# A two-layer decode kernel: three transposing K transfers put ahead of the K loads

## The chip, the cores and the metric

The kernel runs on one core of a Trainium2 chip. The metric is the device time of one execution in microseconds (us). The profile's span runs from the first to the last instruction of a profiled execution and is a little shorter than that execution's device time.

The engines are named as in the profile: PE (TensorE matmul), PEld (its weight load), DVE (VectorE), ACT (ScalarE), POOL (GpSimd), SP (SyncE). SP computes nothing here; it issues every DMA of the kernel, and "SPq" in the profile is its queue. The transfers themselves run on the core's 16 DMA engines.

## The reference

Four sequences (B = 4) of one token each go through two layers, and both layers use the same weights and the same caches. A layer is grouped-query attention over a cache of 4096 positions, and then a gated unit:

```
x = x + A(layernorm(x))      # q = x wq ; softmax(q K^T / sqrt(128)) V ; o wo
x = x + B(layernorm(x))      # (sigmoid(x w_gate) * (x w_up)) w_down
x = x + A(layernorm(x))
x = x + B(layernorm(x))
```

There are 32 query heads and 8 K/V heads of 128 elements, D = 512, F = 1792, all in bf16. One K/V head of one sequence is 4096 x 128 bf16, which is 1 MB for K and 1 MB for V. The caches hold 32 such pairs, 64 MB in all, and layer two needs every one of them again.

## The kernel before

A **unit** is one (layer, sequence, K/V head). Units are worked in pairs: `seq` holds 64 units and the main loop at the end of the kernel runs over `plan`, one pair at a time. SBUF has `NSLOT = 12` **slots** of 1 MB (128 partitions x 4096 bf16). Each slot holds the K or the V of one unit. A K unit is loaded with row p of the slot holding positions 32p to 32p+31; DVE then turns it in place, in blocks of 32x32 words of 32 bits (`k_turn`, L923); `scores` (L940) multiplies the turned slot with the spread queries. `smax`, `spread_max` and `softmax` (L956, L965, L975, L983) make the probabilities, `ptrans` (L1000 to L1032) turns them, `pv` (L1048) multiplies them with V, and `wo_pair` (L1098) with the output weights. Some units of layer one stay in their slots for layer two (`RET`); the others are loaded a second time, so 104 slot loads are made.

All DMAs go out from SP in the order of the list `loads`. `pump()` takes the first free slot (`free`, a list that starts as 0 to 11) for each K or V load, and returns when no slot is free; weights (`wo`, `wg`, `wu`, `wd`) are in the same list and need no slot. Ahead of `loads` stand the load of x and four loads of wq (L394), 1 MB each. A small recorder (`_Sched`) derives the waits: whoever writes a key such as `s9` (slot 9) waits for its last writer and all its readers. A wait of a DMA is a wait of SP, and whatever stands behind it in SP's order waits too. Every slot has its own semaphore (`d0` to `d11`).

The order on SP at the start is: x, wq0 to wq3, K into slots 0 to 4, V into slot 5, one block of wo (512 KB), K into slot 6, V into slot 7, wo, two blocks of wg, K into slot 8, V into slot 9, wo, two blocks of wg, K into slot 10, V into slot 11. Only then do slots come round again.

At the start the compute engines do what needs no K: layernorm, masks, the query matmuls (L621, which wait for wq). Then DVE turns the first two K units, and behind the second turn on DVE stands the scaling of the queries (L632), which the first scores need.

Of the kernel before, what the change touches and what calls it, by code (L numbers as in the profile page):

```python
# [185 lines left out]
def bass_interleave_layers__gqa_block_cached__glu_gated_glu__decode_kernel(  # L186
# [17 lines left out]
    P = 128  # L204
# [4 lines left out]
    NJ = SK // P  # L209
# [12 lines left out]
    S = _Sched()  # L222
# [4 lines left out]
    def sbt(shape, dtype, name):  # L227
        cnt[0] += 1
        return es.enter_context(nc.sbuf_tensor(f"{name}_{cnt[0]}", list(shape), dtype))
# [4 lines left out]
    slot = [sbt([P, NJ * DH], dt.bfloat16, f"slot{i}") for i in range(NSLOT)]  # L234
# [127 lines left out]
    def pump():  # L362
        while loads:
            kind, n = loads[-1]
            if kind in wparts:
                loads.pop()
                dst, src = wparts[kind](n)
                S.dma("sp", (lambda dst, src: lambda e: e.dma_start(dst, src))(dst, src), f"wo{n}" if kind == "wo" else kind, writes=[f"{kind}{n}"])  # L368
                continue
            if not free:  # L370
                return
            loads.pop()
            s = take()
            _, b, u = seq[n]
            if kind == "k":
                where["kn", n] = s
                src = A_k_cache[b, u].rearrange("(p j) d -> p (j d)", p=P)
            else:
                where["v", b, u] = s
                src = A_v_cache[b, u].rearrange("(p j) d -> p (j d)", p=P)  # L380
            dst = slot[s][:, :]
            S.dma("sp", (lambda dst, src: lambda e: e.dma_start(dst, src))(dst, src), f"d{s}", writes=[f"s{s}"])  # L382
# [8 lines left out]
    for k in range(KD):  # L391
        S.dma(
            "sp",
            (lambda k: lambda e: e.dma_start(wq_sb[:, k, :], A_wq[k * P:(k + 1) * P, :]))(k),  # L394
            f"wq{k}",
            writes=[f"wq{k}"],
        )
    pump()

# [4 lines left out]
        writes=["pe0"],  # L404
    )
    dve(lambda e: e.transpose(pidx[:, :], iota_f[:, 0:32]), writes=["pe0"])
    for a in range(4):
# [6 lines left out]
            writes=[f"ident{a}"],  # L414
# [5 lines left out]
    for k in range(KD):  # L420
# [13 lines left out]
        writes=[f"x{b}" for b in range(Bn)],  # L434
# [705 lines left out]
    for b in range(Bn):  # L1140
        n = vstep[last[0, b]] - 1
# [155 lines left out]
```

## Time and profile before

| What | Value |
|---|---|
| median of 2 runs | 324.73 us (323.7 to 325.76) |
| profiled execution, device time | 326.53 us |
| its span | 324.7 us |
| mean granted TensorE clock | 0.686 of full speed |
| PE / DVE / ACT busy | 70% / 58% / 45% of the span |
| bytes moved by DMA | 123.63 MB, mean 381 GB/s |
| DMA queue of SP (q1) | 94.1% of 16 engines' span |
| slot loads | 56 of V and 48 of K, 1 MB each |

The busy shares are averages over stages with different limits. The row of the DMA queue counts the time that the packets took on the 16 engines. In the profile's slices each digit is a tenth of busy time in one of 40 equal parts of the span, some 8.1 us each.

### The profile page before, as it was taken

To read this page: it belongs to the slowest core of one execution; us is meant where nothing else is said; L and a number is where in the kernel's file an instruction comes from. 1 tells how busy PE (TensorE), PEld (TensorE's weight loads), DVE (VectorE), ACT (ScalarE), POOL (GpSimd) and SP (SyncE) were. 2 spreads that over 40 slices of the span, in tenths; PEclk is the share of its full clock that TensorE was granted. 3 is DMA by queue.
4 is the path that set the end of the run, shared out by engine and by line. 5 is a ranking of instruction groups with operands and counts; after the bars stand their busy time and mean duration, and the time that the engine had idled before them with its cause. 6 is when DMAs were issued, how large, how long until landed. Compare 5 with 4: busy or idle time off the path is not lost.

```text
span 324.7 us, 10428 instructions
## 1 busy us (share of the span) xinstructions
PE 227.0 (70%) x4408; PEld 157.4 (48%) x4408; DVE 188.0 (58%) x441; ACT 145.4 (45%) x600; POOL 12.8 (4%) x36
## 2 busy tenths in 40 slices
PE   1345523008197998768798986799797869878975
PEld 1313312006156465546556564464565646455865
DVE  6387343304656458865647696674886467475243
ACT  1005421205045276655435765543676653377620
POOL 0000000000000010000001000000100000010000
PEclk9999999999996655555765555555655555675555
DMA  7999999999999999999999999999999999999800
GB/s 277 428 422 411 401 404 400 401 386 390 400 406 376 339 376 425 418 422 418 410 370 377 417 424 421 421 388 380 377 421 419 420 422 422 417 416 419 369 18 3
DMA packets 22814, 123.63 MB, mean 381 GB/s; under 512 B 2024, under 2 KB 7920, under 8 KB 8944
## 3 DMA queue, kind: packets, MB, share of 16 engines
q1 hardware_dynamic: 22768, 122.96, 94.1%
q8 instruction: 35, 0.57, 0.7%
q14 instruction: 11, 0.09, 0.1%
HBM read 122.95 MB, written 0.00 MB: 379 GB/s over the span
## 4 chain that ended last, share of the span: by engine, by line
DMA 29%; PE 24%; issue 22%; DVE 12%; SPq 11%; ACT 1%; POOL 0%; DVEq 0%; POOLq 0%
DMA slot<-in_A_v_cache_dram 19%; PE O_ps L1048 7%; DVE slot L923 7%; SPq L382 6%; DMA wo<-in_A_wo_dram 5%; DMA slot<-in_A_k_cache_dram 5%; SPq L368 4%; PE S_ps L940 4%; PE O_ps L1098 3%; PE MS L965 2%; PE MS L1007 2%; PE M_ps L858 1%; DVE small L956 1%; PE M_ps L809 1%; PE PT L1000 1%
## 5 line engine op out<-in xcount | busy, mean ns | idle before, releaser
L1032 ACT ACTIVATE pT<-PT 32x64 bf16<-32x64 f32 x504 | 108.1, 214 | 55.1 <-PE PT L1000 43.6
L923 DVE STREAM_TRANSPOSE slot<-slot 128x2048 f32<-128x2048 f32 (+1 forms) x61 | 112.3, 1840 | 32.4 <-DMA slot<-in_A_k_cache_dram 32.4
L1048 PE MATMUL O_ps<-pT,slot 128*128 128x4 bf16 x2048 | 62.0, 166 | 26.3 <-DMA slot<-in_A_v_cache_dram 26.3
L1048 PEld LDWEIGHTS O_ps<-pT,slot 128*128 128x128 bf16 x2048 | 63.5, 105 | 29.8 <-DMA slot<-in_A_v_cache_dram 27.2
L940 PE MATMUL S_ps<-slot,qz 128*16 128x512 bf16 x512 | 59.4, 612 | 3.4 <-POOL qz L675 2.3
L983 ACT ACTIVATE pe<-S_ps,small 128x512 bf16<-128x512 f32 x32 | 22.0, 686 | 59.0 <-issue 40.4
L965 PE MATMUL MS<-valid_f,small 128*128 128x64 f32 x64 | 20.6, 422 | 22.4 <-DVE small L956 22.4
L1098 PEld LDWEIGHTS O_ps<-oT,wo 128*128 128x128 bf16 x640 | 19.3, 105 | 28.8 <-issue 28.4
L965 PEld LDWEIGHTS MS<-valid_f,small 128*128 128x128 f32 x64 | 15.0, 291 | 37.6 <-DVE small L956 34.1
L1098 PE MATMUL O_ps<-oT,wo 128*128 128x2 bf16 (+1 forms) x640 | 20.3, 166 | 16.7 <-DMA wo<-in_A_wo_dram 15.6
L956 DVE TENSOR_REDUCE small<-S_ps 128x1 f32<-128x512 f32 x32 | 21.2, 662 | 6.5 <-PE S_ps L940 6.5
L675 POOL TENSOR_TENSOR qz<-qc,small 128x128 bf16<-128x128 bf16 x32 | 12.6, 399 | 280.9 <-ACT qc L661 143.5
L940 PEld LDWEIGHTS S_ps<-slot,qz 128*16 128x16 bf16 x512 | 12.4, 109 | 22.8 <-issue 17.7
L1007 PE MATMUL MS<-head_f,small 128*128 128x8 f32 x64 | 17.9, 353 | 0.0
L1080 DVE TENSOR_TENSOR oT<-O_ps,rden 128x8 bf16<-128x8 f32 x32 | 5.2, 164 | 19.7 <-PE O_ps L1048 17.9
L1007 PEld LDWEIGHTS MS<-head_f,small 128*128 128x128 f32 x64 | 16.4, 314 | 0.0
L1015 DVE RECIPROCAL rden<-MS 128x8 f32<-128x8 f32 x32 | 6.6, 206 | 14.8 <-PE MS L1007 14.8
L975 DVE CUSTOM_DVE_ANT_0 junk<-MS,mask_f,small 128x64 bf16<-128x64 f32 x32 | 8.5, 267 | 11.4 <-PE MS L965 11.4
L1000 PE MATMUL PT<-ident_bf,pe 128*128 128x64 bf16 x128 | 12.0, 231 | 1.9 <-ACT pe L983 1.5
L1112 DVE TENSOR_TENSOR xT<-xT,O_ps 128x4 f32<-128x4 f32 x32 | 3.9, 154 | 16.1 <-PE O_ps L1098 16.0
L809 PE MATMUL M_ps<-wq,xc_bf 128*1 128x512 bf16 x128 | 12.9, 574 | 0.0
L661 ACT ACTIVATE qc<-M_ps 128x128 bf16<-128x128 f32 x8 | 1.9, 280 | 19.5 <-PE M_ps L650 19.5
(79 smaller groups left out, 150.3 us busy)
## 6 DMA issues: line engine op xcount, KB each, us to landing
slot<-in_A_v_cache_dram SPq DMA_DIRECT2D x56, 1024.0 KB, 11.0
slot<-in_A_k_cache_dram SPq DMA_DIRECT2D x48, 1024.0 KB, 11.7
wq<-in_A_wq_dram SPq DMA_DIRECT2D x4, 1024.0 KB, 7.8
wo<-in_A_wo_dram SPq DMA_DIRECT2D x8, 512.0 KB, 15.9
wg<-in_B_w_gate_dram SPq DMA_DIRECT2D x4, 448.0 KB, 14.0
wu<-in_B_w_up_dram SPq DMA_DIRECT2D x4, 448.0 KB, 14.4
wd<-in_B_w_down_dram SPq DMA_DIRECT2D x2, 896.0 KB, 16.6
row<-in_A_x_dram SPq DMA_DIRECT2D x1, 4.0 KB
```

The costliest lines, as they stand in the source:

```text
L382: S.dma("sp", (lambda dst, src: lambda e: e.dma_start(dst, src))(dst, src), f"d{s}", writes=[f"s{s}"])
L809: (lambda k, st: lambda e: e.matmul(M_ps[h][32 * st:32 * st + 1, :], lhsT=xc_bf[:, k, 0:1], rhs=wv[:, k, h, :, st, :], start=(k == 0), sto ...
L923: dve(lambda e: e.transpose(kf, kf), writes=[f"s{st}"])
L940: (lambda t, b2, e_, c, r0, ul: lambda e: e.matmul(S_ps[p][r0:r0 + 4 * REP, :], lhsT=qz_sb[p][:, ul, t, :, :].rearrange("p a r -> p (a r)" ...
L956: lambda e: e.tensor_reduce(rm_sb[p], S_ps[p][:, :], AX.X, ALU.max),
L965: lambda e: e.matmul(MS[:, 0:16 * REP], lhsT=rm_sb[p].broadcast_to([P, P]), rhs=valid_f[:, :], start=True, stop=True),
L983: lambda e: e.activation(pe_sb[p].rearrange("p j m -> p (j m)"), S_ps[p][:, :], ACTF.Exp, bias=nm_sb[p], scale=exp_scale, accum_out=sm_sb[ ...
L1000: (lambda j: lambda e: e.matmul(PT[:, j * 64:(j + 1) * 64], lhsT=pe_sb[p][:, j, :], rhs=valid_bf, start=True, stop=True))(j)
L1007: lambda e: e.matmul(MS[:, 64:64 + 2 * REP], lhsT=sm_sb[p].broadcast_to([P, P]), rhs=head_f[:, :], start=True, stop=True),
L1032: (lambda dst, frm: lambda e: e.activation(dst, frm, ACTF.Copy))(dst, frm),
L1048: (lambda x, c, j: lambda e: e.matmul(O_ps[p][:, ul * REP:(ul + 1) * REP], lhsT=vv[:, x * JG + c * 4 + j, :], rhs=pT_sb[p][:, x, j, 2 * ul ...
L1098: (lambda c, r: lambda e: e.matmul(O_ps[p][:, 64 + 2 * c:64 + 2 * c + nb], lhsT=wo_sb[:, u * REP + r, c * P:(c + 1) * P], rhs=oT_sb[n][:, ...
```

## The change

Between the four loads of wq and the first `pump()`, three DMAs are added on SP:

```diff
@@ -394,6 +394,16 @@
             (lambda k: lambda e: e.dma_start(wq_sb[:, k, :], A_wq[k * P:(k + 1) * P, :]))(k),
             f"wq{k}",
             writes=[f"wq{k}"],
+        )
+    for n, s in enumerate((9, 10, 11)):
+        S.dma(
+            "sp",
+            (lambda n, s: lambda e: e.dma_start_transpose(
+                slot[s].rearrange("d (j p) -> d j p", j=NJ),
+                A_k_cache[n, 7].rearrange("(p j) d -> p (j d)", p=P),
+            ))(n, s),
+            f"d{s}",
+            writes=[f"s{s}"],
         )
     pump()
```

Each reads the K of head 7 of sequence 0, 1 or 2 from HBM, 1 MB, and writes it turned into slot 9, 10 or 11: for each of the 32 column blocks j, element (p, d) of the source goes to partition d, place p. [...] Nothing reads what they write. The three slots are loaded over by ordinary loads later: V into slot 9, K into slot 10, V into slot 11. Through the recorder those three loads get a wait for `d9`, `d10` and `d11` that they did not have. All other instructions, their order on each engine, and all later loads are the same; behind the insertion their line numbers are 10 higher.

## The prediction

> **What bounds the kernel now.** I read the slices first, then the DMA queue, then the waits, then the start in order of time. The slices and the queue, from the page of the profile:
>
> ```profile
> PE   1345523008197998768798986799797869878975
> PEclk9999999999996655555765555555655555675555
> DMA  7999999999999999999999999999999999999800
> q1 hardware_dynamic: 22768, 122.96, 94.1%
> ```
>
> The reader should see that the DMA row is full from the second slice to the 38th, whereas PE has many low digits in the first ten: in that stretch the compute engines wait for bytes. A kernel whose DMA engines are full has no idle place for 3.1 MB more. That it is the bytes that are waited for, the list of waits says (us in total, times, longest), on the compute engines and then on SP's queue:
>
> ```profile
> DVE slot L923 <- DMA slot<-in_A_k_cache_dram: 32.4, 14, 4.8
> PE O_ps L1048 <- DMA slot<-in_A_v_cache_dram: 26.3, 11, 7.0
> PE O_ps L1098 <- DMA wo<-in_A_wo_dram: 15.6, 1, 15.6
> ...
> SPq L178 <- PE S_ps L940: 72.3, 15, 13.4
> ```
>
> The last line is the other side: SP stands up to 13.4 us before a load because no slot is free. So there are stretches in which the supply runs ahead of the work, and one has to ask whether a delay at the start disappears there. The start itself, from the timeline (start, length, engine, what):
>
> ```profile
> 1.17 2.00 SPq L394 DMA_DIRECT2D wq<-in_A_wq_dram  x4
> 3.21 2.44 SPq L382 DMA_DIRECT2D slot<-in_A_k_cache_dram  x5
> 6.97 8.58 SPq L382 DMA_DIRECT2D slot<-in_A_k_cache_dram  x1
> 13.49 3.55 PE L621 MATMUL M_ps<-xc_bf,wq 128*128 128x4 bf16 x128 [5.93 <-DMA wq<-in_A_wq_dram]
> 15.87 2.31 DVE L923 STREAM_TRANSPOSE slot<-slot 128x2048 f32<-128x2048 f32 x1 [4.80 <-DMA slot<-in_A_k_cache_dram]
> 22.37 1.88 PE L940 MATMUL S_ps<-slot,qz 128*16 128x512 bf16 x16 [0.86 <-POOL qz L675]
> ```
>
> SP has issued everything up to the first wo by 6.97 us and is then held 8.58 us inside one issue: its queue is full, so at the start SP is far ahead and the DMA engines set the pace. wq lands by 13.49, the first K by 15.87, and the first turn starts that moment. The first scores at 22.37 hang on the two turns, since DVE has the query scaling (L632) behind the second.
>
> **The change, part by part.** It removes nothing and moves nothing on PE, DVE, ACT or POOL. It adds three instructions on SP, three transfers of 1,048,576 B on the DMA engines, and three waits on SP.
>
> *The transfers.* The profile of before has no transposing transfer, so I bound one by the rows that move the same bytes in packets of different sizes. Two stretches are nearly pure, the first in 8 KB packets (K and V), the second in 1 KB packets (wd and wo):
>
> ```profile
> 140.00:150.00 10.00, 8.40 (x190) 6.70 (x190) 4.12 (x10) 5.27 (x23) 0.40 (x1) 0.50 1.02 421
> ...
> DMA packets 1663, 1.78 MB, mean 357 GB/s; under 512 B 32, under 2 KB 1647, under 8 KB 1647
> ```
>
> The first line is the windows' row for 140 to 150 us: DMA share 1.02, 421 GB/s. The second is the DMA view for 71 to 76 us. From the first, one engine moves 421/16 = 26.3 GB/s, and an 8192 B packet takes 311 ns. In the second, 1647 - 32 = 1615 packets are of 1 KB and 16 of 8 KB; 16 engines x 5 us = 80 us, less 16 x 0.311, over 1615, gives 46.5 ns for 1024 B. The 7168 B between the two sizes cost 264.5 ns, 27.1 GB/s, which leaves 8.7 ns for each packet whatever its size.
>
> The lower bound takes the three transfers at the 8 KB rate: 3.146 MB / 421 GB/s = 7.5 us. Packets of 1 KB would make 64 per engine and transfer, 64 x 46.5 ns = 3.0 us, 8.9 us for three. The change's view has runs of 128 elements, 256 B, on both sides: 4096 runs, 256 per engine, each an estimated 256/27.1 + 8.7 = 18.1 ns, so 4.6 us per transfer and 13.9 us for three. [...] I take the middle of the two small-packet prices, **11.4 us**, and keep 7.5 and 13.9 as the ends of the rate alone.
>
> [...]
>
> *Issue on SP.* An ordinary 1 MB issue takes 0.33 to 0.48 us on SP when the queue has room. For a transposing one there is no row. wq's 4 MB are in flight until 13.49, ten us after SP reaches the new instructions at 3.21, so that is their cover; price nothing. Without cover: if SP is held until each transfer has landed, the DMA engines stand empty between transfers. The shortest time from issue to landing of a 1 MB load is 5.1 us, 2.5 of it bytes, so a gap is about 2.6 us, three make 7.8, and the top of the cost is 13.9 + 7.8 = 21.7 us.
>
> *The waits.* SP waits for `d9` at the V load into slot 9, the 14th DMA after the transfers, in the profile issued at 28.15, behind some 11 MB of other loads. The transfers would land by about 13.5 + 11.4 = 25 us, and that V load itself moves to about 39 us. Cost nothing. If the transfers were late, every later load stands behind this wait, and the price would be the lateness itself, already in the transfers' bound.
>
> *What the delay does next.* K0 lands 11.4 us later, at 27.3 us; then the turns, the scaling and the scores follow as before, at 33.8 us. PE's query matmuls stay at 13.49 and were not the last to arrive. From there both sides of the kernel, supply and work, are shifted alike. The place where the shift could vanish is SP's 13.4 us wait for a slot, 81.45 to 94.94 us, ended by the scores at 92.96. Just ahead of it the timeline has
>
> ```profile
> 73.01 0.99 PE L1098 MATMUL O_ps<-oT,wo 128*128 128x1 bf16 x32 [15.59 <-DMA wo<-in_A_wo_dram]
> 89.63 1.01 PE L1048 MATMUL O_ps<-pT,slot 128*128 128x4 bf16 x32 [4.57 <-DMA slot<-in_A_v_cache_dram]
> ```
>
> so the work that frees the slot itself stood 4.57 us for bytes: the slot comes free later by the same amount, and nothing is made good. Later stretches (337 GB/s at 100 to 110 us, 376 at 160 to 170) are short of 421 because the work was late there, and the work is now as much later.
>
> *Sum.* Span 324.7 + 11.4 = 336.1 us; the profiled execution's device time 326.53 would become 337.9. That execution lies 1.8 us above the median of the runs, so against 324.73 I forecast **336.1 us**. A measurement here can tell about 2% (6.5 us) from no change.
>
> **The rivals.**
>
> *Swallowed by the slot waits.* If the supply's lead at 81 to 95 us is real slack, the delay is gone by 95 us and the time is 324.7 to 331 us. For it: SP's 13.4 us wait, and the shortfall in GB/s behind it, (421 - 337) / 421 x 10 = 2.0 us at 100 to 110, 1.3 at 110 to 120, and 1.1 at 160 to 170, 4.4 us in which the engines could catch up. Against it: PE's wait to 89.63. It decides if the work, not the bytes, sets that scoring; with all 4.4 us made good, 11.4 leaves 7.0, 331.7, and with the 7.5 us price 3.1, **327.8 us**, not slower by what can be told. This is the case on the other side. A gain has no mechanism but the clock: PEclk is full until 100 us and halves when PE fills up; a later and sparser start might carry the full clock through more of the work. I see no row for it beyond that.
>
> [...]
>
> *Block by block.* The 96 blocks of 128x128 go one after another, each with a round trip of its own. The nearest row is the 4 KB store at the end, issued at 323.03 for 0.29 us, with the span ending at 324.7: 1.38 us from issue to landing. 96 x 1.38 = 132 us, **457 us**. Against it: everything else in this profile is pipelined, 22,768 packets in 324.7 us. [...]
>
> **How the numbers follow.** The forecast, a shift by 7.5 to 21.7 us that is passed on, has 0.78; swallowed 0.14, of which 0.02 for a gain over 2%; small pieces 0.06; block by block 0.02. The range takes in the forecast's ends, 332.2 and 346.4, and a little of the swallowed case: 331 to 346 us. Slower by over 2% is 0.78 + 0.06 + 0.02 = 0.86, within 2% 0.12, faster 0.02.
>
> **What would show it.** Right: the three new DMAs take 2.5 to 4.6 us of the engines each, DVE's first L923 (now L933) starts near 27 us with DMA full ahead of it, the first scores near 34, and every later landmark (the end of SP's long slot wait at 94.94, the last V landing) about 11 us later. Wrong in the rate: the first turn far from 27. Wrong in the passing on: the first turn late by 11, but the scores at 92.96 or the end late by much less. A span that grows by more than the first turn does would mean a cost that I have not seen.

## The result and the profile after

The changed kernel takes 345.02 us (344.56 to 345.49, two runs) against 324.73 before (323.7 to 325.76): ratio 1.0625, 95% interval 1.0468 to 1.0783. It is slower, by more than the 11.4 us forecast and inside the range given. A second comparison, with more runs of both kernels on one chip, gave 342.33 us against 327.39: 1.0482, interval 1.0415 to 1.0548. The 327.39 belongs to the same unchanged kernel, so a difference of 15 us and one of 20 are the same finding within what executions differ. One execution of the version with twelve quarters, 349.68 us, was in a slower state than the others and is left out of its median below.

From the page of the profile after, the rows that were shown of before:

```profile
PE   1300353140627899867998988498985959889975
PEclk9999999999999995555556555565655555665555
DMA  7999999999999999999999999999999999999900
GB/s 280 334 185 361 424 396 405 405 402 405 376 403 412 386 353 351 420 422 418 419 412 358 360 419 422 418 397 356 367 392 425 376 419 422 420 390 421 412 20 4
q1 hardware_dynamic: 35152, 126.11, 94.2%
```

The DMA row is as full as before, but the GB/s row has a hole in its third slice: 185 GB/s where the kernel before had 422. q1 carries 12,384 packets more: 12,288 of data, which is three times 4096 runs of 256 B, and 96 small ones beside them. The busy digit of that slice is 9 all the same; one has to read the two rows together.

The start, from the timeline (start, length, engine, what):

```profile
1.15 2.00 SPq L394 DMA_DIRECT2D wq<-in_A_wq_dram  x4
3.20 22.88 SPq L401 DMA_TRANSPOSE slot<-in_A_k_cache_dram  x3
13.80 3.55 PE L631 MATMUL M_ps<-xc_bf,wq 128*128 128x4 bf16 x128 [6.23 <-DMA wq<-in_A_wq_dram]
26.12 2.79 SPq L382 DMA_DIRECT2D slot<-in_A_k_cache_dram  x5
31.43 2.31 DVE L933 STREAM_TRANSPOSE slot<-slot 128x2048 f32<-128x2048 f32 x1 [20.34 <-DMA slot<-in_A_k_cache_dram]
38.03 1.88 PE L950 MATMUL S_ps<-slot,qz 128*16 128x512 bf16 x16 [0.86 <-POOL qz L685]
```

SP is held for 22.88 us inside the three new issues and reaches the first K load at 26.12, where before it was there at 3.21. The first turn starts at 31.43 instead of 15.87, 15.6 us later, and the first scores at 38.03 instead of 22.37, 15.7 later. Stretches of 2 us (length, busy of five engines, clock, DMA share, GB/s) show what the DMA engines did meanwhile:

```profile
14.00:16.00 2.00, 2.00 (x81) 2.00 (x79) 0.00 (x0) 0.00 (x0) 0.00 (x0) 1.00 1.28 290
16.00:18.00 2.00, 1.35 (x51) 1.27 (x48) 0.00 (x0) 0.00 (x0) 0.00 (x0) 1.00 0.71 161
18.00:20.00 2.00, 0.00 (x0) 0.00 (x0) 0.00 (x0) 0.00 (x0) 0.00 (x0) 1.00 1.15 177
20.00:22.00 2.00, 0.00 (x0) 0.00 (x0) 0.00 (x0) 0.00 (x0) 0.00 (x0) 1.00 1.28 290
22.00:24.00 2.00, 0.00 (x0) 0.00 (x0) 0.00 (x0) 0.00 (x0) 0.00 (x0) 1.00 0.94 121
24.00:26.00 2.00, 0.00 (x0) 0.00 (x0) 0.00 (x0) 0.00 (x0) 0.00 (x0) 1.00 0.92 198
```

While a transposing transfer runs, its bytes go at a steady 290 GB/s: 3.146 MB / 290 = 10.8 us. In the stretches that hold a change from one to the next, 16 to 20 and 22 to 26 us, the rate is 121 to 198. The delay of 15.6 us is therefore 10.8 us of bytes and 4.8 us of what I call **dry time** below: time in which the engines move less than they can. The name says nothing of the cause; packets are in flight in part of it, as the DMA share shows (1.15 at 18 to 20 us, 0.94 at 22 to 24, 0.92 at 24 to 26).

That the delay is passed on, the waits say. SP's longest wait for a slot is 13.1 us where it was 13.4 and ends at 110.27 instead of 94.94, 15.3 us later. The matmul that stood 4.57 us for V ahead of it, at 89.63, now stands at 104.89. From the list of waits (us in total, times, longest), and then from the timeline:

```profile
DVE slot L933 <- DMA slot<-in_A_k_cache_dram: 49.4, 13, 20.3
SPq L178 <- PE S_ps L950: 71.1, 15, 13.1
```

```profile
104.89 1.02 PE L1058 MATMUL O_ps<-pT,slot 128*128 128x4 bf16 x32 [4.56 <-DMA slot<-in_A_v_cache_dram]
```

The wait for K has grown by 17.0 us, 15.5 of it in one piece: its longest was 4.8 and is 20.3. The span is 343.4 us, 18.7 more than 324.7, so 3 us come later on: the maxima over the scores (L956 before, L966 after) stand 15.9 us later at pair 16, 17.0 at pair 18 and 18.8 at pair 24.

### The profile page after: what moved, and what is told of

Same layout as the page of the kernel before. It is cut to its first block, busy times and chain, and to the rows that moved or that the text cites. A ratio compares the mean times of both kernels' runs of the same rounds, so it can differ in the third digit from the quotient of the medians.

```text
span 343.4 us, 10431 instructions
## 1 busy us (share of the span) xinstructions
PE 229.0 (67%) x4408; PEld 157.7 (46%) x4408; DVE 188.5 (55%) x441; ACT 145.9 (42%) x600; POOL 12.8 (4%) x36
## 3 DMA queue, kind: packets, MB, share of 16 engines
q1 hardware_dynamic: 35152, 126.11, 94.2%
HBM read 122.95 MB, written 0.00 MB: 358 GB/s over the span
## 4 chain that ended last, share of the span: by engine, by line
DMA 26%; PE 25%; issue 21%; SPq 15%; DVE 12%; ACT 1%; POOL 0%; DVEq 0%; POOLq 0%; ACTq 0%
DMA slot<-in_A_v_cache_dram 16%; PE O_ps L1058 7%; DVE slot L933 7%; SPq L401 7%; DMA slot<-in_A_k_cache_dram 5%; DMA wo<-in_A_wo_dram 5%; PE S_ps L950 4%; SPq L382 4%; SPq L368 4%; PE O_ps L1108 3%; PE MS L975 2%; PE M_ps L819 2%; DVE small L966 2%; PE MS L1017 2%; PE PT L1010 1%
## 5 line engine op out<-in xcount | busy, mean ns | idle before, releaser
L950 PE MATMUL S_ps<-slot,qz 128*16 128x512 bf16 x512 | 60.3, 620 | 3.5 <-POOL qz L685 2.5
L975 PEld LDWEIGHTS MS<-valid_f,small 128*128 128x128 f32 x64 | 15.4, 299 | 39.2 <-DVE small L966 35.8
L1108 PE MATMUL O_ps<-oT,wo 128*128 128x2 bf16 (+1 forms) x640 | 20.3, 165 | 16.6 <-DMA wo<-in_A_wo_dram 15.6
L966 DVE TENSOR_REDUCE small<-S_ps 128x1 f32<-128x512 f32 x32 | 21.3, 665 | 7.8 <-PE S_ps L950 7.8
L1017 PE MATMUL MS<-head_f,small 128*128 128x8 f32 x64 | 17.6, 349 | 0.0
L660 PE MATMUL M_ps<-qT,ident_bf 128*32 128x32 bf16 (+1 forms) x80 | 1.7, 205 | 20.0 <-DVE qT L642 19.2
## 6 DMA issues: line engine op xcount, KB each, us to landing
wo<-in_A_wo_dram SPq DMA_DIRECT2D x8, 512.0 KB, 15.9
wg<-in_B_w_gate_dram SPq DMA_DIRECT2D x4, 448.0 KB, 15.1
wu<-in_B_w_up_dram SPq DMA_DIRECT2D x4, 448.0 KB, 14.1
```

What stands on the lines that cost most here:

```text
L950: (lambda t, b2, e_, c, r0, ul: lambda e: e.matmul(S_ps[p][r0:r0 + 4 * REP, :], lhsT=qz_sb[p][:, ul, t, :, :].rearrange("p a r -> p (a r)" ...
L966: lambda e: e.tensor_reduce(rm_sb[p], S_ps[p][:, :], AX.X, ALU.max),
L975: lambda e: e.matmul(MS[:, 0:16 * REP], lhsT=rm_sb[p].broadcast_to([P, P]), rhs=valid_f[:, :], start=True, stop=True),
L1017: lambda e: e.matmul(MS[:, 64:64 + 2 * REP], lhsT=sm_sb[p].broadcast_to([P, P]), rhs=head_f[:, :], start=True, stop=True),
L1108: (lambda c, r: lambda e: e.matmul(O_ps[p][:, 64 + 2 * c:64 + 2 * c + nb], lhsT=wo_sb[:, u * REP + r, c * P:(c + 1) * P], rhs=oT_sb[n][:, ...
```

## The experiments

The theory after the two traces: 10.8 us of bytes in 256 B packets, 4.8 us of dry time because SP is held within each transposing issue, all passed on; the last 3 us are differences between executions. "First turn" is DVE's first turn of a K slot (15.87 before), "end" the profiled span (324.7 before) or the median against the runs of before on the same chip.

**The changed kernel once more.** No edit.

> The changed kernel once more, beside the other versions. Theory (the three transfers cost 10.8 us of bytes at 290 GB/s and 4.7 us in which the DMA engines run dry, and the 15.6 us at the start are passed on; the further 3 us of the first profile come from single late loads and change from execution to execution): 15 to 19 us over the kernel before, first turn at 31.4 us, with the places of the further 3 us elsewhere than at pairs 18 and 24. Rival (the further 3 us belong to the change): again 19 to 20 us, lost at the same pairs.

342.33 us against 327.39. The first turn is at 31.20, the span 340.4, and the 15.5 us at pair 0 are 15.6 at the last pair. At pairs 18 and 24, where the first profile lost 0.8 and 2.1 us, this one loses 0.2 and 0.1; at pair 26 it loses 1.3. The further 3 us did not come back, so nothing ties them to the change.

**Three plain loads of the same bytes.**

```diff
-            (lambda n, s: lambda e: e.dma_start_transpose(
-                slot[s].rearrange("d (j p) -> d j p", j=NJ),
+            (lambda n, s: lambda e: e.dma_start(
+                slot[s][:, :],
```

> Three ordinary loads of the same 1 MB each, 8 KB rows, in place of the three transposing ones. Theory (bytes at 421 GB/s, SP not held, nothing runs dry): first turn 7.5 us later than before, at 23.4, and the whole about 7.5 us longer. Rival (any three loads ahead of K cost a delay that the slot waits swallow in part): the first turn 7.5 us late, but the end late by less than 5.

334.85 us against 327.39, 1.0246 (1.0186 to 1.0307): 7.5 us longer, as the bytes say.

```profile
24.58 2.31 DVE L933 STREAM_TRANSPOSE slot<-slot 128x2048 f32<-128x2048 f32 x1 [13.50 <-DMA slot<-in_A_k_cache_dram]
```

The first turn is 8.7 us late, 1.2 more than the bytes; at pair 2 the delay is 7.35, so that 1.2 is gone two pairs later; it may come from how the first K loads share the engines, which is not shown. Nothing is swallowed: the last pair is 8.4 us late. So a plain megabyte costs 2.5 us here, and the transposing one twice that.

**Three plain loads in runs of 256 B.**

```diff
+            (lambda n, s: lambda e: e.dma_start(
+                slot[s].rearrange("q (j d) -> q j d", j=NJ),
+                A_k_cache[n, 7].rearrange("(j q) d -> q j d", q=P),
```

> Three ordinary loads, but in runs of 256 B on both sides: 4096 packets each, as the transposing ones have, without the transpose. Theory (the engines set the 290 GB/s by the packet size; SP is not held as in a transposing transfer): 256 packets per engine at 14.1 ns, 10.8 us for three, first turn at 26.7, the end 10.8 us later. Rival 1 (packets cost 18 ns each, and the transposing transfer has a saving of its own): 13.9 us, first turn at 29.8. Rival 2 (4096 packets hold SP's issue and the engines run dry between transfers whatever their kind): 15.6 us as in the changed kernel.

341.49 us against 327.39, 14.1 longer; the first turn at 30.95, 15.1 late. The theory missed. By the first turn alone the second rival (31.4) is nearer than the first (29.8); the flow decides for the first, which has the mechanism. The DMA view for 13 to 22 us and a stretch of the windows:

```profile
DMA packets 1962, 2.00 MB, mean 222 GB/s; under 512 B 23, under 2 KB 1961, under 8 KB 1961
```

```profile
18.00:20.00 2.00, 0.00 (x0) 0.00 (x0) 0.00 (x0) 0.00 (x0) 0.00 (x0) 1.00 1.12 221
```

The trace records packets of 1 KB here (1938 of 512 B to 2 KB in that view), so four runs as one. At 217 to 221 GB/s one such packet passes on each engine every 75 ns, 18.7 ns for a run of 256 B, close to the 18.1 ns that the prediction worked out from the 8 KB and 1 KB stretches. Up to 21.7 us the rate has one short dip in that view, to 196 to 209 GB/s for 0.9 us from 19.5; SP spends 0.84 us on the first issue and is held for 10.82 and 5.65 us in the second and third. So plain small runs were slower here but hardly ever dry, and transposing ones were faster (14.1 ns per 256 B) but dry in between. In this place the two cost almost the same, 15.1 and 15.6 us, for different reasons. One difference is not separated here: this version picks its runs of 256 B from HBM at a distance of 32 KB, whereas the source rows of the transposing transfers lie in pieces of 8 KB. So 18.7 against 14.1 ns compares two ways of reading as well as two kinds of transfer.

**Each transposing transfer followed by one K load.**

```diff
             S.dma("sp", ..., f"d{s}", writes=[f"s{s}"])
+            if extra:
+                turned(*extra.pop())
...
+    turned(0, 9)
+    extra.extend([(2, 11), (1, 10)])
     pump()
```

(`turned(n, s)` is the added DMA as a function; `...` stands for what is left out.)

> The same three transposing transfers on SP, but each followed by one K load: wq, transposing, K0, transposing, K1, transposing, K2, and so on. Theory (a transposing transfer needs some 1.7 us after SP reaches it before its bytes flow, and SP is held until its descriptors are nearly through, so between two of them the engines run dry; a plain 2.5 us load between them covers that): about 11 to 13 us over the kernel before instead of 15.6. Rival (each transposing transfer takes 5.3 us whatever stands ahead of it): 15 to 16 us, as in the changed kernel.

343.35 us against 327.39, 16.0 longer; the span is 341.0 and the delay 15.3 us at pair 2 and 15.7 at pair 6. The rival held, and with it fell the place that I had given the dry time. SP's queue and the windows:

```profile
15.51 0.57 SPq L384 DMA_DIRECT2D slot<-in_A_k_cache_dram  x1
16.12 7.15 SPq L405 DMA_TRANSPOSE slot<-in_A_k_cache_dram  x1
23.32 0.58 SPq L384 DMA_DIRECT2D slot<-in_A_k_cache_dram  x1
```

```profile
16.00:18.00 2.00, 1.17 (x44) 1.08 (x41) 0.00 (x0) 0.00 (x0) 0.00 (x0) 1.00 1.24 194
...
20.00:22.00 2.00, 0.00 (x0) 0.00 (x0) 0.30 (x1) 0.00 (x0) 0.00 (x0) 1.00 0.94 205
...
24.00:26.00 2.00, 0.00 (x0) 0.00 (x0) 0.01 (x1) 0.00 (x0) 0.00 (x0) 1.00 1.06 197
```

SP comes out of the first transposing issue at 15.46 (in the changed kernel at 15.4, about 1.4 us before that transfer's rate falls from 294 to 49 GB/s, at 16.75). The K load that it issues next has moved little by 18: there is a hole behind the transposing transfer, 194 GB/s at 16 to 18 us and 197 at 24 to 26 behind the second, with a K load next as with a transposing one, and 385 GB/s come only at 18 to 20. In the changed kernel the first load of wq, issued at 1.15, has its first bytes at about 2.15 us, 1.0 us later. Of the 0.39 MB that moved here from 16 to 18 us, an estimated 0.22 MB belong to the transposing transfer (290 GB/s up to 16.75, as in the changed kernel); the other 0.17 MB are 0.4 us at 385 GB/s, as if the K load, issued at 15.51, had begun at 17.6, an estimated 2.1 us later. So the hole is not only SP's lateness. The second transposing transfer also starts slowly, with 205 GB/s at 20 to 22. The plain load between cures neither.

**The transposing transfers on ACT's queue.**

```diff
     ln_a(0, Bn)
+    for n, s in enumerate((9, 10, 11)):
+        turned(n, s, "act")
+    pump()
     ln_b(Bn)
```

(and the first `pump()` goes away.)

> The same three transposing transfers, issued by ACT right behind its conversion of the normalised x, so that SP goes on issuing plain loads beside them. Theory (10.8 us of the delay is the engines' time for the bytes, and some 4 to 5 us are dry time, because SP, held inside a transposing issue until 1.4 us before its last byte, has nothing queued behind it and the next transfer needs 2 us and more from its issue to its bytes): with plain loads on another queue nothing runs dry, and the end is 10 to 12 us later than before. Rival (a transposing transfer occupies the engines for 5 us by itself, dry or not): 15 us. ACT is held too, so its first copy of the queries (L661 before) comes late, by as much as 8 us, which the theory says costs nothing, since the loads go on.

345.5 us against 326.05, 19.5 longer. Neither had it; the experiment doesn't tell the two apart, for reasons of its own. From the timeline and the list of waits, and from the DMA view for 15 to 35 us:

```profile
6.73 56.87 ACTq L401 DMA_TRANSPOSE slot<-in_A_k_cache_dram  x3
64.46 1.89 PE L949 MATMUL S_ps<-slot,qz 128*16 128x512 bf16 x16 [42.23 <-POOL qz L684]
SPq L382 <- DMA slot<-in_A_k_cache_dram: 33.9, 3, 16.4
```

```profile
q1 hardware_dynamic: 1463, 7.27, 94.7%
q10 hardware_dynamic: 1463, 0.37, 10.0%
```

ACT is held for 56.87 us, and its copy of the queries, which the first scores need, waits behind: scores at 64.46 instead of 22.37. Nor does SP go on beside it: its loads into slots 9, 10 and 11 wait for the transposing transfers into these slots, 33.9 us in three waits, the longest from 29.57 to 45.99 (the rate falls to 217 GB/s at 55 to 65 us). This is the case of late transfers that the prediction named, in which every later load stands behind `d9`. In the changed kernel, SP has no such wait.

q10 is ACT's queue, q1 SP's: in the 20 us in which both have work, each moved 1463 packets, yet the one 0.37 MB and the other 7.27. In this stretch the queue of small packets got as many of them through as the queue of large ones, and hardly any bytes. From 25 to 45 us it is 2043 packets on q1 and 3004 on q10, with 7.01 and 0.77 MB, so one to one is the count of the first stretch alone. My line that the late copy of the queries "costs nothing" was wrong: it reckoned with 8 us, and the first scores came 42 us late.

**One transposing transfer instead of three.** `enumerate((9, 10, 11))` becomes `enumerate((9,))`.

> One transposing transfer in place of three. Theory (each costs its 3.6 us of bytes and about 1.5 us of dry time behind it): first turn 5 us later than before, the end 5 us later. Rival (there is a fixed cost of 4 to 5 us for turning the queue from plain to transposing and back, paid once however many there are): 8 us.

332.14 us against 326.05, 1.0177 (1.0133 to 1.0221), 6.1 longer; the first turn at 21.93, 6.1 late; 5.0 at pair 2 and 4.85 at the last. The theory's 5 us is nearer than 8; a fixed cost of 4 to 5 us for the turning back and forth is out.

**The three moved behind the first six slot loads.** As in the run with K between, but all three are issued after V into slot 5.

> The same three transposing transfers on SP, moved behind the first six slot loads (K into 0 to 4, V into 5). Theory (the DMA queue sets the pace from 2 us to the end of the loads, so the place of the 15.6 us does not matter): first turn at 15.9 us as before, and the end 14 to 16 us later. Rival (the delay hurts because it stands ahead of the first K, which nothing covers; later on the loaded slots cover a part): the end less than 10 us later.

345.19 us against 326.05, 19.1 longer. The first turn is at 15.88, as before, and pairs 0 and 1 are on time; then the delay is 15.1 us at pair 2, 16.2 at pair 3, 17.0 at pair 6, and 19.5 at the end, more than the 14 to 16 expected. So the cost is not saved at this place, where the queue sets the pace as well: K first in line gains nothing. From pair 6 on the delay is 1 to 5 us more than in the second profile of the changed kernel; at the end it is 0.8 us more than in the first. I did not follow that up.

**Six halves and twelve quarters.** Each transfer is cut along the column blocks:

```diff
+        for h in range(2):
...
+                    slot[s].rearrange("d (j p) -> d j p", j=NJ)[:, 16 * h:16 * h + 16, :],
+                    A_k_cache[n, 7].rearrange("(p j) d -> p (j d)", p=P)[:, 16 * h * DH:(16 * h + 16) * DH],
```

> The same bytes in six transposing transfers of half the size (16 of the 32 column blocks each). Theory (the dry time belongs to each transfer, the bytes do not change): 10.8 us of bytes and six dry times of about 1.5 us, first turn 19 to 21 us later than before, the end as much. Rival (the loss goes with the bytes, as a lower rate): 15.6 us as in the changed kernel.

344.15 us against 326.05, 18.1 longer; the first turn at 34.62, 18.75 late, just under the 19 to 21 expected. The bytes are the same, three transfers more cost 3.2 to 3.4 us more: at these sizes the dry time goes with the number of transfers, about 1.1 us each.

> The same bytes in twelve transposing transfers of 256 KB each. Theory (the same law, 10.8 + 1.3 + 12 x 1.1): 25.3 us later at the first turn, at 41.2, and the end 24 to 27 us later. Rival (SP is held because the queue is full, and at 64 packets per engine a transfer lets SP go at once, so that the next one is being prepared while this one runs): less dry time than with six, first turn between 31 and 35.

343.87 us against 326.94, 16.9 longer; the first turn at 34.73, 18.9 late, just as with six. Here the law broke, and the rival's range holds, though not its less dry time than with six. The two views by source line, halves first, then quarters (duration on SP: min, median, max in ns):

```profile
L403 SPq DMA_TRANSPOSE slot<-in_A_k_cache_dram x6: 2690/2974/10242, 3.2 to 25.7; - x6
```

```profile
L403 SPq DMA_TRANSPOSE slot<-in_A_k_cache_dram x12: 1310/1403/5918, 3.3 to 26.8; - x12
```

With 128 packets per engine SP is held 2.97 us, with 64 it is free after 1.40. Twelve times 1.40 is 16.8 us, more than the 10.8 us of the bytes, and only the first two issues fall into the time in which wq still drains. A price of 1.1 us per transfer therefore holds here for the transfers of 0.5 MB and more only; that SP's issue sets the pace of those of 256 KB is what these rows suggest.

**The same bytes in one transposing transfer of 3 MB.** Slots 9 to 11 become one tensor, and the source is three heads in a row:

```diff
+        lambda e: e.dma_start_transpose(
+            last3.rearrange("d (j p) -> d j p", j=3 * NJ),
+            A_k_cache[0, 5:8].rearrange("u s d -> (u s) d").rearrange("(p j) d -> p (j d)", p=P),
+        ),
```

> The same number of bytes in one transposing transfer of 3 MB (K of heads 5 to 7 of sequence 0) into slots 9 to 11, which lie side by side here; the loads over the three slots all wait for it. Theory (first turn delayed by 14.1 ns per 256 B packet and engine, 10.8 us in all, plus 1.3 us once, plus 1.1 us for each transposing transfer; that law fits the runs with one, three and six transfers): 13.2 us later at the first turn, at 29.1, and the end 12 to 14 us later. [...]

340.29 us against 326.94, 1.043 (1.0353 to 1.0508), 13.4 longer; the span 337.7, 13.0 longer.

```profile
29.23 2.31 DVE L934 STREAM_TRANSPOSE slot<-slot 128x2048 f32<-128x2048 f32 x1 [18.16 <-DMA slot<-in_A_k_cache_dram]
```

```profile
18.00:20.00 2.00, 0.00 (x0) 0.00 (x0) 0.00 (x0) 0.00 (x0) 0.00 (x0) 1.00 2.07 286
20.00:22.00 2.00, 0.00 (x0) 0.00 (x0) 0.00 (x0) 0.00 (x0) 0.00 (x0) 1.00 0.61 96
22.00:24.00 2.00, 0.00 (x0) 0.00 (x0) 0.00 (x0) 0.00 (x0) 0.00 (x0) 1.00 1.28 290
```

The first turn is at 29.23, forecast 29.1, and 2.1 us earlier than with the same bytes in three. The one hole, at 20 to 22 us in the middle of the transfer, comes with a single packet of the instruction queue (q8, 0.02 MB) in the DMA view for 19.5 to 21 us. That the one causes the other is not shown. The changed kernel's second change of transfer, at 22 to 25 us, has the hole (116 GB/s) and no packet of that queue, so the holes between transfers do not all come from it.

## Why the prediction was right or wrong, point by point

**What bounds the kernel: right.** The DMA queue sets the pace from 2 us to the end of the loads. Three plain megabytes cost their bytes (7.5 us), and the three transposing ones cost as much or more behind the first six loads as they do ahead of K.

**The rate of the transfers: right in size, partly by luck.** The term was 11.4 us between 7.5 and 13.9; it measured 10.8, at 290 GB/s. But 11.4 was the middle of a price for 1 KB packets and one for 256 B packets. The data packets of these transfers have 256 B (12,288 for 3.15 MB), for which the prediction's own price was 13.9. That estimate, 18.1 ns for a 256 B packet, is near what the plain runs showed (18.7 ns); transposing ones ran at 14.1. Nor do the runs of 256 B follow from the view, as the prediction has it: in memory both sides go on for 8 KB, and it is the trace that shows packets of 256 B. With the dry time, three transfers in 15.6 us make 202 GB/s.

**Issue on SP: wrong.** This is the step that failed. It priced the issue at nothing, under the cover of wq's 4 MB. The cover serves the first transfer alone: SP is held in it until 15.4, in the next two for 5.3 us each, and each later one has no cover but what the one before has left. By 1, 3 and 6 transfers, the delay of the first turn less the bytes is 2.5, 4.5 to 4.8, and 7.9 us: 1.4 once and 1.1 for each transfer; some 1.2 of the once is in the plain loads too. With twelve transfers this law no longer holds. The prediction did have this mechanism, as the top of its range (2.6 us for each, 7.8 for three), and left it out of the sum. The runs show the size of the term, not its whole cause: with K loads put between, the holes stay. By the prediction's own signs a first turn far from 27 meant a wrong rate; it came at 31.4, and the rate was right and this term was missing. With 4.8 us in it, the sum would have been 16.2 us and the forecast 340.9, against 345.02 and 342.33 measured.

**The waits on `d9` to `d11`: right.** The V load into slot 9 is issued at 42.39 (forecast 39), and the transposing transfer into that slot has landed by 17.4, 14.2 us after its issue. Nothing stands behind it.

**The delay passed on: right.** 15.6 us at the first turn, 15.3 at the end of the long slot wait, PE's wait for V ahead of it 4.56 us where it was 4.57.

**The rivals.** Swallowed by the slot waits: out, the seven plain microseconds arrive at the end as well. The gain by the clock: PEclk now is full for 15 slices of 8.6 us, where it was 12 of 8.1, so the full clock did last longer (mean 0.714 against 0.686; over all executions 0.711 to 0.728 against 0.680 to 0.714), yet no gain is left at the end: the last pair is 15.6 to 18.6 us late. Small pieces, given 0.06, and block by block: out, the packets are of 256 B, and 96 blocks pass in 10.8 us of flow, 0.11 us each.

**Left open.** Why a transposing transfer comes to its 290 GB/s only some 2.5 us after the one ahead has fallen from them (in the changed kernel from 16.75 to 19.2 us and from 22.0 to 24.7), whether moving them back in itself costs more, how much of 18.7 against 14.1 ns comes from the order in which the source is read, and whether the packet of the instruction queue makes the hole in the 3 MB transfer. Whether plain loads on a second queue can fill the dry time, the run on ACT could not tell.

## What to carry to other kernels

Price a DMA with short runs by its packets, from two stretches of the trace with packets of different size (here 18.1 ns for 256 B, where plain runs took 18.7 and transposing ones 14.1), and then ask what stands behind it in its queue: here a 1 MB transposing transfer held its issuer until about 1.4 us before its rate fell, a dry time of about 1.1 us each came on top, and one transfer of 3 MB was cheaper than three of 1 MB (first turn 13.4 us late against 15.6). In this kernel, whose DMA queue is busy for 94.1% of the span, bytes added at either of two places were added to the end (14.9 to 20.3 us ahead of K, 19.1 behind the first six loads). Before transfers go to another queue, ask which loads wait for them: on ACT's queue they came late, with ACT held for 56.87 us, and SP stood 33.9 us behind them. An upper bound that has a mechanism and a row behind it belongs in the sum, if the cover that is named against it covers only the first of several.

## What the runs showed that I had not expected

- Transposing transfers flowed at 290 GB/s in 256 B packets, 14.1 ns each per engine, faster than a plain load that picked runs of 256 B at a distance of 32 KB (217 to 221 GB/s).
- In 20 us two queues moved 1463 packets each: on q10, the queue of the transposing transfers, they came to 0.37 MB, beside 7.27 MB on q1, and the engine that issues the former was held for 56.87 us.
- The page's HBM read is 122.95 MB before and after the change, though q1 moved 3.15 MB more after it (126.11 against 122.96): the bytes that the three transfers added are missing from that line, so bytes are better read from the queue's row.
